# A gated attention/MLP decode step on one core: the first load of w1 split between two DMA queues

## The chip, the core and the metric

The kernel runs on one core of a Trainium2 chip. The core has TensorE (matmul), VectorE, ScalarE, GpSimd (POOL in the profile) and SyncE (SP), and 16 DMA engines that move data between HBM and SBUF. Two queues issue its loads: SyncE's (q1 in the profile) and ScalarE's (q10). The metric is the device time of one execution in microseconds (us), and of several executions the median.

## What is computed

One decode step for two sequences: attention over a cache of 4,096 keys for 32 heads of 128, a small ReLU MLP on the same input, and a sigmoid gate that mixes the two. All tensors are bf16. Cut to what matters:

```python
# A_x [2,1,512], k_cache and v_cache [2,32,4096,128], wq [512,4096], wo [4096,512]
# w1 [512,1376], w2 [1376,512], gate_w [512]
x = A_x
g = sigmoid((x * gate_w).sum(-1, keepdims=True))
q = (x @ wq) split into 32 heads
p = softmax(q . k_cache * 128**-0.5)
a = (p . v_cache) @ wo
b = relu(x @ w1) @ w2
return g * a + (1 - g) * b
```

The caches are 128 MiB of the 145 MB that are read; wq and wo are 4 MiB each, w1 and w2 some 1.4 MB each.

## The kernel before, in words

**SBUF.** The tensor `kv` has three regions of 64 KB in each of the 128 partitions (`NREG`, `REG`). Each of the two caches is cut into eight units of 8 MiB that fill one region; in a load of a unit each partition is one row of 65,536 B. The third region (`C`) holds, until the queries are made, the weights wq (32,768 B in each partition) and w1 (11,008 B in each partition: four of the 512 rows of w1, so that partition p has rows 4p to 4p+3), an identity matrix, and in its first three partitions x (two rows of 1,024 B) and gate_w (one).

**Order of the work.** `P` collects operations for each engine in lists; `emit` writes them out in order, each with its waits on semaphores ahead of it. A DMA adds 16 to its semaphore when all of it has landed. SyncE's list is: w1 (L235), wq (L236), the units k0 and k1 without waits, then k2 into region C (L250, after "pe_qh", "dve_setup" and "act_q", that is, once the weights there are used), and then one unit after the other, each waiting until the region that it goes into is free. The order of the units is k0 to k4, v0, k5, v1, k6, v2, k7, v3 to v7. v7 comes in two pieces (L246); w2's last 1,280 rows (L252) and wo in four pieces (L255) follow, and at the end the store of the output (L257). ScalarE's list begins with x (L233) and gate_w (L234); its only other load is w2's first 96 rows, of 1,024 B each (L663), during the v units.

**The start.** GpSimd makes the constants (L262 to L265). `gate` transposes x and gate_w on TensorE (L284, waits for both loads), ScalarE copies them to `xT32` (L287, the signal "act_xT"), four matmuls and a few small operations make the gate. `x_proj` (L340 to L378) waits for "act_xT", wq and w1 (L371) and multiplies x by wq and w1 in one loop on TensorE (L320 clears, L314 matmuls); its end is "pe_qh". VectorE and ScalarE put the queries into place ("act_q"), and GpSimd builds from them the weights for the key matmuls (`w_block`, L393). The key units wait for these: `k_turn` (L404) transposes a unit in place on VectorE once it has landed, and TensorE multiplies it (L314).

**The end.** `project` (L598) multiplies by wo piece by piece as it lands, VectorE and ScalarE cast the result (L623, L625), and SyncE stores it. `fill` puts operations without effect (increments of a semaphore that nobody waits for) into an engine's list ahead of `project`; they set how many instructions the engine has up to there.

**Blocks.** The program is emitted in two parts: a first few operations of SyncE, ScalarE and GpSimd (4, 2 and 4, the tuple `rest` at L700), then TensorE's whole list with its loops, then what is left of the others.

## Time and profile before

| | us |
|---|---|
| median of 3 runs (lowest to highest) | 342.52 (342.45 to 342.62) |
| the profiled execution, its own time | 342.64 |
| its span in the profile | 341.3 |
| busy: TensorE matmul / weight load | 209.9 / 33.9 |
| busy: VectorE / ScalarE / GpSimd | 155.4 / 13.9 / 41.8 |
| w1: from issue to landing | 5.8 |
| wq: from issue to landing | 15.0 |
| w2's first 96 rows: from issue to landing | 19.8 |

How to read the profile: times are microseconds from the span's start, L12 is line 12 of the kernel. A line of the timeline gives the start, the duration, the engine, the line, the operation and how many of it, and in brackets how long the engine was idle before it and what ended that. SPq and ACTq are the DMA queues of SyncE and ScalarE; their durations are those of the issue, not of the transfer. In the table by stretches, each engine's busy time and count is followed by the clock granted to TensorE, the share of the 16 DMA engines and GB/s. The trace also has a record of every DMA packet (queue, size, start, duration), without the number of the DMA engine that moved it.

### The profile page before, as it was taken

What the parts mean: (1) busy time and instruction counts of PE and PEld (TensorE: products, weight loads), DVE (VectorE), ACT (ScalarE), POOL (GpSimd) and SP (SyncE); (2) the same over time, 40 slices, a digit from 0 to 9 for tenths busy, and PEclk for the clock granted to TensorE, in tenths of its full rate; (3) what the DMA queues carried; (4) which work ended last, traced back from release to release, by engine and by line L of the source; (5) the groups of instructions that cost most, each with busy time, mean ns of one, the idle gap of its engine ahead of it and who ended that gap; (6) DMA issues with size and microseconds to landing.
All of it is one profiled execution on the core that took longest, in us unless ns stands there. A gap on an engine that the chain in (4) does not pass through costs nothing. (4 is left out here: it accounts for less than half of the span.)

```text
span 341.3 us, 3101 instructions
## 1 busy us (share of the span) xinstructions
PE 209.9 (61%) x1243; PEld 33.9 (10%) x843; DVE 155.4 (46%) x45; ACT 13.9 (4%) x37; POOL 41.8 (12%) x53
## 2 busy tenths in 40 slices
PE   0080079685968909972995059820993773718387
PEld 0040011000100101110111001100100100101024
DVE  1010897979799769229800693019805000000111
ACT  2001000000000020000000000000003000000000
POOL 1000000000000004005002300050000235050400
PEclk9999999999898965996799559965696659676789
DMA  8998989898999999998989898989999999999896
GB/s 346 434 492 369 492 369 492 369 492 369 492 392 468 399 461 445 415 484 376 492 369 492 369 492 369 492 369 492 392 468 392 468 438 424 398 441 461 374 440 264
DMA packets 3580, 145.46 MB, mean 426 GB/s; under 512 B 405, under 2 KB 634, under 8 KB 762
## 3 DMA queue, kind: packets, MB, share of 16 engines
q1 hardware_dynamic: 3460, 145.33, 98.7%
q10 hardware_dynamic: 118, 0.10, 0.1%
q8 instruction: 1, 0.02, 0.0%
q14 instruction: 1, 0.01, 0.0%
HBM read 145.43 MB, written 0.00 MB: 426 GB/s over the span
## 5 line engine op out<-in xcount | busy, mean ns | idle before, releaser
L404 DVE STREAM_TRANSPOSE kv<-kv 128x8192 uint32<-128x8192 uint32 (+1 forms) x17 | 138.6, 8186 | 74.4 <-DMA kv<-in_A_k_cache_dram 74.4
L314 PE MATMUL PS<-kv,zero 128*128 (+1 forms) x544 | 130.3, 421 | 40.4 <-PEq L481 40.4
L314 PE MATMUL PS<-kv,ptw 128*32 x512 | 48.1, 469 | 11.7 <-issue 11.5
L320 PE MATMUL PS<-zero 32*128 32x512 bf16 (+2 forms) x21 | 9.7, 537 | 57.6 <-ACT zero L410 20.3
L449 POOL TENSOR_TENSOR ptw<-E,mask 128x512 bf16<-128x512 bf16 x32 | 32.2, 1038 | 21.1 <-PE PS L314 10.9
L467 DVE TENSOR_TENSOR X<-PS,maskc 128x512 f32<-128x512 f32 x2 | 1.4, 692 | 64.1 <-PE PS L314 64.1
L314 PEld LDWEIGHTS PS<-kv,zero 128*128 (+1 forms) x144 | 13.6, 103 | 154.6 <-issue 154.6
L393 POOL TENSOR_TENSOR zero<-q_sb,mask 128x32 bf16<-128x32 bf16 x8 | 1.9, 251 | 147.0 <-PE PS L314 123.3
L471 POOL TENSOR_TENSOR X<-X,maskc 128x512 f32<-128x512 f32 x6 | 6.2, 1039 | 109.2 <-ACT X L470 109.2
L314 PE MATMUL PS<-X,zero 128*64 128x512 f32 x16 | 11.6, 819 | 12.3 <-PEq L481 12.3
L314 PEld LDWEIGHTS PS<-kv,ptw 128*32 x512 | 8.7, 99 | 50.4 <-issue 49.7
L320 PEld LDWEIGHTS PS<-zero 32*128 32x128 bf16 x21 | 2.1, 109 | 69.4 <-issue 43.7
L373 DVE STREAM_TRANSPOSE ptw<-PS 128x1024 f32<-128x1024 f32 x1 | 1.3, 1251 | 16.4 <-PE PS L320 16.4
L415 DVE TENSOR_REDUCE zero<-PS 128x2 f32<-128x2048 f32 x2 | 4.5, 2271 | 9.1 <-PE PS L314 9.1
L470 ACT ACTIVATE X<-PS 128x512 f32<-128x512 f32 x6 | 3.6, 597 | 71.4 <-PE PS L314 71.4
L422 ACT ACTIVATE nrow<-mmax 128x32 f32<-128x32 f32 x2 | 0.5, 228 | 132.8 <-DVE mmax L419 132.8
L440 DVE STREAM_TRANSPOSE E<-E 128x2048 bf16<-128x2048 bf16 x2 | 4.6, 2300 | 2.4 <-ACT E L430 2.4
L410 ACT ACTIVATE zero<-zero 1x1 f32<-1x1 f32 x9 | 1.8, 200 | 84.9 <-DMA kv<-in_A_v_cache_dram 67.9
L430 ACT ACTIVATE E<-PS,negm 128x1024 bf16<-128x1024 f32 x4 | 4.4, 1109 | 0.6 <-DVE negm L426 0.6
L284 PE MATMUL PS<-kv 3*128 3x3 bf16 x4 | 0.3, 165 | 6.5 <-DMA kv<-in_gate_w_dram 6.5
L598 PE MATMUL PS<-kv,oW 128*2 128x256 bf16 x64 | 4.0, 272 | 0.4 <-DMA kv<-in_A_wo_dram 0.4
L314 PEld LDWEIGHTS PS<-X,zero 128*64 (+1 forms) x16 | 1.8, 161 | 15.8 <-issue 15.6
(49 smaller groups left out, 27.6 us busy)
## 6 DMA issues: line engine op xcount, KB each, us to landing
kv<-in_A_v_cache_dram SPq DMA_DIRECT2D x1, 6144.0 KB, 36.7
kv<-in_A_wq_dram SPq DMA_DIRECT2D x1, 4096.0 KB, 15.0
kv<-in_A_wo_dram SPq DMA_DIRECT2D x1, 2560.0 KB, 35.9
kv<-in_A_v_cache_dram SPq DMA_DIRECT2D x1, 2048.0 KB, 41.3
kv<-in_B_w_dram SPq DMA_DIRECT2D x1, 1376.0 KB, 5.8
kv<-in_B_w_dram SPq DMA_DIRECT2D x1, 1280.0 KB, 30.1
kv<-in_A_wo_dram SPq DMA_DIRECT2D x1, 1024.0 KB, 37.9
kv<-in_A_wo_dram SPq DMA_DIRECT2D x1, 384.0 KB, 38.4
```

The costliest lines, as they stand in the source:

```text
L314: return e.add_instruction(mybir.InstMatmult(name=nc.get_next_instruction_name(), engine=mybir.EngineType.PE, ins=[rhs, lhsT], outs=[e.low ...
L320: return e.matmul(dst, lhsT=nil, rhs=nil.unsqueeze(1).to_broadcast([32, 4, 128]) if n == 512 else nil[:, 0:n], start=not stop, stop=stop, ...
L393: pool(lambda g: g.tensor_tensor(out=out, in0=q, in1=msk, op=ALU.mult), waits=([["act_q", "dve_mask8"], []] + [[f"pesc_{x}"] for x in rang ...
L404: ins = v.transpose(out=reg[:, 4096 * p0:4096 * p1], in_=reg[:, 4096 * p0:4096 * p1])
L410: return lambda a: a.activation(out=tick[:, 2 + i:3 + i], in_=tick[:, 0:1], func=ACT.Copy).then_inc(sem["go"], n)
L415: dve(lambda v: v.tensor_reduce(out=mpad[:, 0:2], in_=PSF[:, 0:2048].rearrange("p (x h q) -> p h x q", h=2, q=16), axis=AX.XY, op=ALU.max) ...
L430: act(lambda a, h=h: a.activation(out=E[:].rearrange("p (x h q) -> p h x q", h=2, q=16)[:, h], in_=PSF[:, 0:2048].rearrange("p (x h q) -> ...
L440: dve(lambda v: v.transpose(out=E[:], in_=E[:]), waits=[f"act_exp{b}"], signal=f"dve_et{b}")
L449: pool(lambda g, src=src, dst=dst: g.tensor_tensor(out=dst, in0=src, in1=msk, op=ALU.mult), waits=(([f"dve_et{b}"] if ub == 0 else []) + ( ...
L470: act(lambda e: e.activation(out=X2[:], in_=src, func=ACT.Copy), waits=[f"pe_v_{v}"], signal=f"act_x_{v}")
L471: pool(lambda e: e.tensor_tensor(out=X, in0=X, in1=msk, op=ALU.mult).then_inc(sem["xg"], 1), waits=[f"act_x_{v}"] + ([] if v else ["dve_se ...
L598: pe(lambda e, g=g: e.matmul(psf(64 * g, 64 * g + 2, FIN_C0, 256), lhsT=w, rhs=m[:, 256 * g:256 * g + 256], start=start, stop=stop, tile_p ...
```

## The change

w1 is loaded by two DMAs instead of one: ScalarE sends partitions 0 to 15, as the first thing in its list and so ahead of x and gate_w, and SyncE sends partitions 16 to 127 where it sent all 128. Both add 16 to w1's semaphore, so `x_proj` waits for 32. One `fill` operation of ScalarE goes, and ScalarE's first part has three operations instead of two.

```diff
+    for q, p0, p1 in ((act, 0, 16), (sp, 16, 128)):
+        q(lambda e, p0=p0, p1=p1: e.dma_start(w1_sb[p0:p1], B_w1.rearrange("(p t) f -> p (t f)", t=4)[p0:p1]).then_inc(sem["w1"], 16))
     act(lambda e: e.dma_start(x_sb[0:2], A_x.rearrange("b s d -> (b s) d")).then_inc(sem["x"], 16))
     act(lambda e: e.dma_start(x_sb[2:3], gate_w.rearrange("(o d) -> o d", o=1)).then_inc(sem["gw"], 16))
-    sp(lambda e: e.dma_start(w1_sb, B_w1.rearrange("(p t) f -> p (t f)", t=4)).then_inc(sem["w1"], 16))
     sp(lambda e: e.dma_start(wq_sb, A_wq.rearrange("(p t) n -> p (t n)", t=4)).then_inc(sem["wq"], 16))
...
-        pe(fn, dwaits=[(sem["wq"], 16), (sem["w1"], 16)], waits=["act_xT"], signal="pe_qh")
+        pe(fn, dwaits=[(sem["wq"], 16), (sem["w1"], 32)], waits=["act_xT"], signal="pe_qh")
...
-    fill("act", 5)
+    fill("act", 4)
...
-    rest = (("sp", nc.sync, 4), ("act", nc.scalar, 2), ("pool", nc.gpsimd, 4), ("dve", nc.vector, 0))
+    rest = (("sp", nc.sync, 4), ("act", nc.scalar, 3), ("pool", nc.gpsimd, 4), ("dve", nc.vector, 0))
```

## The prediction

> **What bounds the kernel now.** I read the page's slices first, then the DMA queues, the end of the chain, and last the first eight microseconds.

> ```profile
> DMA  8998989898999999998989898989999999999896
> GB/s 346 434 492 369 492 369 492 369 492 369 492 392 468 399 461 445 415 484 376 492 369 492 369 492 369 492 369 492 392 468 392 468 438 424 398 441 461 374 440 264
> ...
> q1 hardware_dynamic: 3460, 145.33, 98.7%
> q10 hardware_dynamic: 118, 0.10, 0.1%
> ```

> The 16 DMA engines are busy in every slice; only the first and the last move clearly less. SyncE's queue (q1) alone carries 145.33 MB. No compute engine comes near: TensorE is at 61%, VectorE at 46%. In the trace's packet records one row of 65,536 B takes 2,420 ns (27.08 GB/s per engine), one of 32,768 B 1,213 ns and one of w1's 11,008 B 413 ns. Adding up the records, no engine idles between 3.5 and 336 us. So the time is when the engines start, plus a fixed sum of rows, plus the tail. The tail, in the chain of work that ended last:

> ```profile
> 300.10 37.89 DMA kv<-in_A_wo_dram
> 337.99 0.04 issue
> 338.03 1.64 PE PS L598 x24
> 339.67 0.02 issue
> 339.69 0.41 DVE ptw L623
> ```

> wo's last pieces are waited for, then 24 matmuls, the cast and the store of the output follow. A DMA counts as landed only when all the engines that carry it are done, so the slowest of the 16 sets the end. Since every engine runs without a pause, a delay of the slowest engine at the start reaches the end whole. Hence only the start matters here, first by stretches (the last two columns are the share of the DMA engines and GB/s), then by its issues:

> ```profile
> 0.00:1.60 1.60, 0.00 (x0) 0.00 (x0) 0.00 (x0) 0.00 (x0) 0.84 (x7) 1.00 0.00 0
> 1.60:2.00 0.40, 0.00 (x0) 0.00 (x0) 0.00 (x0) 0.00 (x0) 0.40 (x1) 1.00 1.45 225
> 2.00:3.00 1.00, 0.00 (x0) 0.00 (x0) 0.58 (x4) 0.53 (x1) 0.39 (x1) 1.00 0.48 143
> 3.00:4.00 1.00, 0.00 (x0) 0.00 (x0) 0.70 (x4) 0.75 (x1) 0.00 (x0) 1.00 1.14 484
> ```

> ```profile
> 0.74 0.40 SPq L235 DMA_DIRECT2D kv<-in_B_w_dram  x1
> 0.74 0.54 ACTq L233 DMA_DIRECT2D kv<-in_A_x_dram  x1
> ...
> 1.19 0.42 SPq L236 DMA_DIRECT2D kv<-in_A_wq_dram  x1
> 1.31 0.23 ACTq L234 DMA_DIRECT2D kv<-in_gate_w_dram  x1
> ...
> 6.53 0.26 PE L284 MATMUL PS<-kv 3*128 3x3 bf16 x4 [6.53 <-DMA kv<-in_gate_w_dram]
> ...
> 16.28 1.03 PE L320 MATMUL PS<-zero 32*128 32x512 bf16 x3 [8.94 <-issue]
> ```

> Both queues issue at 0.74. Nothing moves before 1.6. A packet is counted where it starts, so the step from 143 to 484 GB/s means that most first rows are still running until 3 us. By the packet records x's two rows start at 1.67 and 1.68; w1's first rows start at 1.77 to 1.96 on eight engines and 2.2 to 2.73 on the others. Those first rows end between 2.60 and 3.27; from then on each engine puts 413 ns rows end to end. The slowest has w1's eight rows at 6.14. Had it begun with x (1.67) at full pace, its first row would have ended at 2.08: what there is to win is 3.27 - 2.08 = 1.19 us at most.

> **The change, part by part.**

> *Issues.* SyncE still issues one DMA for w1 (112 rows, not 128), so wq and the k units are issued where they were: 0.40 and 0.42 us, then L250. ScalarE issues one DMA more, by the nearest row 0.40 us; x moves to about 1.2 and gate_w to about 1.75, with no wait added. ScalarE's next work, the table load, starts at 2.47 anyway behind POOL's memset: nothing. One no-op fewer in ScalarE's last section keeps its count of instructions.

> *x and gate_w behind a row of w1.* ScalarE's only other load, w2's first 96 rows, shows how the queues mix: issued at 284.7, it appears as six rounds of one 1 KB row per engine, 2.49 us apart, so one row of each queue in turn. x and gate_w can thus lose some rows: 413 ns each beside w1, 1,213 ns beside wq. They have room. The gate runs from 6.53, its casted x is ready at 7.02, and x_proj waits for wq until 16.28: gate_w may come 16.28 - 7.02 = 9.3 us later, whereas the eight wq rows of one engine are 9.7 us. If it came behind all of them, x_proj would begin up to about 1 us later, and that is covered too: q is ready at 26, k0 lands at 35.5 (9 us of room), and the DMA that waits for q (k2, issued at 26.4) is not needed before k1 lands at 54.9. Zero; without this cover, 1 us. The doubled count on w1's semaphore adds nothing, since wq lands last.

> *The rows.* w1's 128 rows are eight per engine. w2's 96 rows came as six per engine. So 16 rows should be one per engine and 112 seven: still eight, 176,128 B from ScalarE plus the rest, no byte more. What changes is which engine writes which partitions. In a 128-row load each engine has eight partitions of its own; with six or seven rows per engine the shares can't coincide with these, so engines meet in one part of SBUF. No row shows two long rows meeting. The nearest is w2's load beside v7: each 1 KB row takes 46 to 52 ns and the 65,536 B row behind it is 20 to 33 ns longer in five of the six rounds, together some 75 ns, twice the 38 ns that 1,024 B take at 27.08 GB/s. [...] That reads as two writers sharing one way at half pace; that all engines show much the same stretch, in the first round only 9 to 16 ns, speaks for a cost of switching queues instead. I take the sharing, by that doubling.

> The bounds for ScalarE's 16 rows: 413 ns if nothing is shared; 8 x 413 = 3.3 us if partitions 0 to 15 have only two ways of eight. I take four writers to a way, between them: 4 x 413 = 1.65 us. SyncE's seven rows: 7 x 413 = 2.89 us with no meeting, 5.78 if each row meets one other; I take the middle, 4.34, for the slowest engine. Start at 1.70 (x's rows): 1.70 + 1.65 + 4.34 = 7.69 against 6.14, so **+1.55 us**. I let the slow first rows of today (0.52 us of stretch and 0.41 of idling, mean per engine) pass beneath the sharing; on top they give +2.5, and seven meetings give +3.0. With no meeting among the seven: 6.24, +0.1.

> [...]

> **Rivals.**

> *Nothing is shared, and ScalarE's short DMA fills the start (not slower).* For it: x's small DMA moved first, 0.10 us ahead of w1 and up to 1.06 ahead of the last engine. Each engine would do a row of 413 ns while SyncE's descriptors are still arriving, and its first SyncE row then ends no later than today's 2.60 to 3.27, with six left instead of seven: 0.41 us less, 342.1; at the very most 1.19 less, 341.3. It decides if a row of 11,008 B takes about 413 ns beside three others into partitions 0 to 15. Against it: first rows were slow on engines that had started early, too (up to 1,362 ns).

> *No net effect.* The engines' start is as slow with two queues, because the first rows wait for memory and not for the queue: 342.5. For it: the eight early and the eight late engines end their first rows in the same stretch. [...]

> **How the numbers follow.** The profiled execution took 342.64 us: span 341.3 and 1.3 around it. It lies 0.12 above the median of 342.52. 342.64 + 1.55 = 344.19 on its own time, 344.1 from the median. Chances: sharing that shows, 0.55 (own range 343.3 to 345.4, the top being 342.5 + 2.9); nothing shared, 0.30, of which 0.13 wins more than 0.2% (0.69 us, about what a measurement of this kernel can tell from no change) and 0.17 less; no net effect, 0.15. So faster 0.13, same 0.32, slower 0.55. The range must reach the rivals: 341.8 to 345.4.

> **What would show it.** In the profile after: w1's 11,008 B rows of ScalarE's queue at about 1,650 ns on all engines, SyncE's w1 rows at 413 or 826, the slowest engine through with w1 near 7.7 instead of 6.1, wq landing 1 to 2 us later than 15.0 after its issue, and the last wo matmuls about 1.5 us later with the tail unchanged. Rows of 413 ns throughout, and GB/s in 2 to 3 us far above 143, would make me wrong; so would a gate that starts after 26 us, or an engine idle after 3.5.

## The result and the profile after

The changed kernel takes 345.37 us (median of 6 runs, 345.06 to 345.82) against 342.57 us (342.45 to 342.74): 2.80 us more, a ratio of 1.0081 with a 95% interval of 1.0070 to 1.0091. Slower was forecast, with 344.1 us.

The profiled execution took 345.54 us, its span is 344.2, so the 1.3 us around it have stayed and the loss lies within. The stretches of the start, from the profile after (last two columns: share of the DMA engines, GB/s):

```profile
1.60:2.00 0.40, 0.00 (x0) 0.00 (x0) 0.00 (x0) 0.00 (x0) 0.40 (x1) 1.00 2.27 330
2.00:3.00 1.00, 0.00 (x0) 0.00 (x0) 0.58 (x4) 0.53 (x1) 0.38 (x1) 1.00 0.33 110
3.00:4.00 1.00, 0.00 (x0) 0.00 (x0) 0.70 (x4) 0.75 (x1) 0.00 (x0) 1.00 1.44 231
```

From 3 us on, where 484 GB/s were counted before, it is 231. The same table for 1.6 to 9 us as a whole, first of the kernel before:

```profile
1.60:9.00 7.40, 0.53 (x8) 0.39 (x8) 1.45 (x8) 2.05 (x5) 0.79 (x1) 1.00 1.01 403
```

and after:

```profile
1.60:9.00 7.40, 0.00 (x0) 0.00 (x0) 1.28 (x7) 1.28 (x1) 0.78 (x1) 1.00 1.07 262
```

The engines' share is as high as before (1.07 and 1.01), so they are not waiting for work: each has a row in hand, and the rows move at two thirds of the rate. The busy share alone does not show the loss here; the GB/s beside it (262 and 403) do. In the timeline after, the consequences downstream:

```profile
0.74 0.39 SPq L235 DMA_DIRECT2D kv<-in_B_w_dram  x1
0.74 0.42 ACTq L235 DMA_DIRECT2D kv<-in_B_w_dram  x1
...
1.19 0.53 ACTq L236 DMA_DIRECT2D kv<-in_A_x_dram  x1
...
10.32 0.26 PE L286 MATMUL PS<-kv 3*128 3x3 bf16 x4 [10.32 <-DMA kv<-in_gate_w_dram]
...
19.23 1.03 PE L322 MATMUL PS<-zero 32*128 32x512 bf16 x3 [8.10 <-issue]
```

The gate starts 3.8 us later than before (10.32 against 6.53) and still has its room. x_proj, which waits for wq, starts at 19.23 instead of 16.28. The DMA issues show the same (KB, us from issue to landing), after:

```profile
kv<-in_A_wq_dram SPq DMA_DIRECT2D x1, 4096.0 KB, 18.0
```

By the packet records the slowest engine is through with w1 at 8.79 us instead of 6.14, so **2.65 us** later; the first wq row of each engine is stretched, too (1,413 to 1,731 ns, not 1,213), and wq ends at 18.69 instead of 15.82 (+2.87). From there the distance stays: k0 ends 2.9 us later, the last of wo 3.0. The end of the chain, after:

```profile
338.58 2.35 PE PS L600 x40
340.93 0.04 issue
340.98 1.62 PE PS L600 x24
342.59 0.03 issue
342.62 0.41 DVE ptw L625
```

The last 24 matmuls begin at 340.98 instead of 338.03 and take as long as before.

### The profile page after: what moved, and what is told of

Read it like the earlier page. It is cut to its first block, busy times and chain, and to the rows that moved or that the text cites. A ratio compares the mean times of both kernels' runs of the same rounds, so it can differ in the third digit from the quotient of the medians.

```text
span 344.2 us, 3101 instructions
## 1 busy us (share of the span) xinstructions
PE 208.8 (61%) x1243; PEld 33.8 (10%) x843; DVE 155.4 (45%) x45; ACT 13.9 (4%) x37; POOL 41.8 (12%) x53
## 5 line engine op out<-in xcount | busy, mean ns | idle before, releaser
L316 PE MATMUL PS<-kv,ptw 128*32 x512 | 47.0, 458 | 12.9 <-issue 12.8
```

The costliest lines, as they stand in the source:

```text
L316: return e.add_instruction(mybir.InstMatmult(name=nc.get_next_instruction_name(), engine=mybir.EngineType.PE, ins=[rhs, lhsT], outs=[e.low ...
```

## The experiments

Theory A: an engine that writes into partitions which another engine is filling shares one way into SBUF with it, and both go slower ("way" stands for whatever it is that they share). Rival B: two queues that feed the same engines disturb each other at the start. Rival C: the cost comes from the memory side, the extra DMA or the narrow shape. All kernels below start from the kernel before; `w1_in` is w1 as `(p t) f -> p (t f)`, and w1's semaphore is awaited to 32 where two DMAs add to it. Differences are between medians, against the runs of the kernel before on the same chip (342.56 to 342.65).

### The queue or the partitions: sp_both and columns

```diff
 # sp_both
+    for p0, p1 in ((0, 16), (16, 128)):
+        sp(lambda e, p0=p0, p1=p1: e.dma_start(w1_sb[p0:p1], w1_in[p0:p1]).then_inc(sem["w1"], 16))
 # columns
+    act(lambda e: e.dma_start(w1_sb[:, 0:688], w1_in[:, 0:688]).then_inc(sem["w1"], 16))
     act(lambda e: e.dma_start(x_sb[0:2], ...
+    sp(lambda e: e.dma_start(w1_sb[:, 688:], w1_in[:, 688:]).then_inc(sem["w1"], 16))
```

> w1 still in 16 and 112 rows, but both from SyncE's queue, ScalarE as before the change. Theory A (rows of several engines meet on one way into SBUF): the queue doesn't matter, w1's rows are stretched to 500 to 1,500 ns again and the time is 2.3 to 3.1 us above before (344.9 to 345.7). Theory B (two queues that feed the same engines disturb each other at the start): the time goes back to before, 342.4 to 342.8.

> ScalarE sends an eighth of w1 ahead of x again, but as the first 1,376 B of all 128 rows; SyncE sends the other 9,632 B of all 128. Bytes, queues and order as in the changed kernel, each engine stays with its own eight partitions. Theory A: no stretch beyond the first rows, 342.0 to 342.9 (eight more packets of some 8 ns per engine; perhaps a fuller start). Theory B: 344.5 to 345.5, as in the changed kernel.

sp_both: 344.82 us, +2.21 (ratio 1.0063, 1.0050 to 1.0077). columns: 342.72 us, +0.11 (1.0003, 0.9994 to 1.0012). The stretch from 1.6 to 9 us, first of sp_both:

```profile
1.60:9.00 7.40, 0.53 (x8) 0.39 (x8) 1.45 (x8) 2.05 (x5) 0.79 (x1) 1.00 1.08 328
```

and of columns:

```profile
1.60:9.00 7.40, 0.00 (x0) 0.00 (x0) 1.28 (x7) 1.28 (x1) 0.79 (x1) 1.00 1.02 403
```

One queue with the split by partitions loses; two queues with a split by columns, the same bytes and the same order, move 403 GB/s as before. B falls as the cause of this loss. sp_both came out 0.1 below its expected range and 0.6 below the changed kernel, so where the 16 rows stand in the order has some weight. columns also answers the hope behind the other rival: ScalarE's first row starts at 2.76 us, a microsecond behind SyncE's (1.75), and there is no gain.

### The 16 rows alone: copies into spare space

Here w1 is loaded whole as before, and its first 16 rows (176 KB) once more, into space that nothing reads. This leaves the 112 rows out of the question and costs one row of bytes per engine, 0.41 us.

```diff
+    spare = kv[:, C, 22528:28032]
+    act(lambda e: e.dma_start(spare[0:16], w1_in[0:16]).then_inc(sem["w1"], 16))       # copy_16
+    act(lambda e: e.dma_start(spare[0:128:8], w1_in[0:16]).then_inc(sem["w1"], 16))    # copy_16_apart
+    act(lambda e: e.dma_start(spare[0:32:2], w1_in[0:16]).then_inc(sem["w1"], 16))     # copy_16_pairs
+    act(lambda e: e.dma_start(spare[:, 0:688], w1_in[0:16].rearrange("p (c f) -> (p c) f", c=8)).then_inc(sem["w1"], 16))  # copy_128
```

> The kernel before, and ScalarE loads the first 16 rows of w1 a second time, ahead of x, into spare space of partitions 0 to 15. These are 176 KB more, one row of 413 ns per engine, so at least +0.41 us. Theory A with four engines to a way: 4 x 413 = 1.65 us, so 344.0 to 344.6. Theory B: +0.41 and whatever two queues cost, which is the same for this kernel and the next one.

> As copy_16, but the 16 rows go to every eighth partition (0, 8, ... 120) instead of 0 to 15; HBM addresses, queue, row length and number of rows are the same. [...] Theory B, and any cause on the side of HBM or of the descriptors: the same time as copy_16.

> Control for the copies: the same 176 KB of w1 a second time from ScalarE ahead of x, but laid out as 1,376 B in each of all 128 partitions. Theory A: bytes alone, 0.41 to 0.6 us above before (343.0 to 343.3). If the extra bytes themselves, or an extra DMA ahead of x, made copy_16's 2.83 us: 345.

> copy_16 with the 16 rows in every second partition (0, 2, ... 30). How large is a way? [...] If a way is eight partitions in a row, four meet: 344.2 to 344.6, and copy_16 had eight (3.3 us), copy_16_apart none.

| kernel | partitions | us | difference | ratio, 95% |
|---|---|---|---|---|
| copy_128 | all, 1,376 B each | 343.12 | +0.56 | 1.0017, 1.0008 to 1.0027 |
| copy_16_apart | every 8th | 343.56 | +0.95 | 1.0026, 1.0017 to 1.0036 |
| copy_16_pairs | every 2nd of 0 to 30 | 343.72 | +1.16 | 1.0037, 1.0023 to 1.0050 |
| copy_16 | 0 to 15 | 345.44 | +2.83 | 1.0080, 1.0067 to 1.0094 |

Queue, HBM addresses and bytes are the same in all four. The moment is not: by the packet records the copied rows start at 2.73 us in copy_16 and at 2.82 in copy_128, but only at 5.16 in copy_16_apart and 5.33 in copy_16_pairs, where ScalarE's issue took 0.58 and 0.59 us instead of 0.41. So copy_128 and copy_16, which move at nearly the same moment, are the pair to compare: the extra DMA and its bytes cost 0.56 us over all partitions (rows of 1,376 B) and 2.83 in 16 neighbouring ones (rows of 11,008 B). How much of the distance from copy_16 to copy_16_apart is owed to the partitions and how much to the moment, these two don't tell; no run has separated rows that move at 2.7 us. And copy_16 costs well over 1.65 us, the author's estimate for four engines to a way.

### Away from the start: copy_16_late and copy_16_apart_late

The same two copies, issued by ScalarE behind the copy that gives "act_xT", into the stream of wq.

```diff
     act(lambda a: a.activation(out=xT32[:, :, 0:3], ... signal="act_xT")
+        act(lambda e: e.dma_start(spare[0:16], w1_in[0:16]).then_inc(sem["w1"], 16))       # or spare[0:128:8]
```

> copy_16 with its DMA issued by ScalarE only after x is transposed (at about 7 us), into the running stream of wq. Theory A with four to a way and no help from the slow start: 1.65 us (344.3), and up to copy_16's 2.8 if the owners of the ways are held up as well. If copy_16's cost belongs to the start (first rows, filling of the queues): 0.41 to 0.6 above before (343.0 to 343.2).

> copy_16_late with the 16 rows in every eighth partition, the cleanest pair without the start. [...] No meeting: 343.0.

copy_16_late: 344.27 us, +1.71 (1.0052, 1.0038 to 1.0065). copy_16_apart_late: 343.68 us, +1.03 (1.0031, 1.0019 to 1.0043). The first is near the author's estimate of four engines to a way, 4 x 413 ns = 1.65; the second is 0.62 above the 0.41 us of its bytes. Here the moment is the same, too (the first copied row starts at 10.59 us in both), so the 0.68 us between them belong to the partitions; the row length and the narrow shape are the same in both, and with that C falls. The two intervals overlap a little; the single runs lie at 344.23 to 344.46 and 343.52 to 344.24 (the trace of the second is of its slowest, 344.24). The view by stretches, where the copies pass, first of the kernel before:

```profile
10.00:11.00 1.00, 0.00 (x0) 0.00 (x0) 0.00 (x0) 0.00 (x0) 0.00 (x0) 1.00 1.21 524
11.00:13.00 2.00, 0.00 (x0) 0.00 (x0) 0.00 (x0) 0.00 (x0) 0.00 (x0) 1.00 0.72 311
13.00:14.20 1.20, 0.00 (x0) 0.00 (x0) 0.00 (x0) 0.00 (x0) 0.00 (x0) 1.00 1.01 437
```

and of copy_16_late:

```profile
10.00:11.00 1.00, 0.00 (x0) 0.00 (x0) 0.00 (x0) 0.00 (x0) 0.00 (x0) 1.00 0.68 209
11.00:13.00 2.00, 0.00 (x0) 0.00 (x0) 0.00 (x0) 0.00 (x0) 0.00 (x0) 1.00 1.01 246
13.00:14.20 1.20, 0.00 (x0) 0.00 (x0) 0.00 (x0) 0.00 (x0) 0.00 (x0) 1.00 1.02 437
```

Less from 10 to 13 us, then 437 GB/s as before: the loss is local, and no later row repairs it. In the packet records the 16 rows themselves take only 413 to 819 ns. The wq row of 32,768 B **behind** each takes 1,918 to 2,324 ns instead of 1,213; the two together are 2.67 to 2.74 us on every engine, 1.1 more than 413 + 1,213. So most of the added time is not written at the 16 rows but at the rows next behind them. In copy_16 it is written at the rows of w1 behind: the 16 that start between 4.0 and 5.2 us take 1,340 to 1,628 ns each instead of 413.

### The 112 rows: copy_112 and late_16

```diff
 # copy_112: rows 16 to 127 once more, into spare space, ahead of x
+    act(lambda e: e.dma_start(spare[16:128], w1_in[16:128]).then_inc(sem["w1"], 16))
 # late_16: the change's two parts, but ScalarE's DMA stands behind "act_xT"
+    sp(lambda e: e.dma_start(w1_sb[16:128], w1_in[16:128]).then_inc(sem["w1"], 16))
+        act(lambda e: e.dma_start(w1_sb[0:16], w1_in[0:16]).then_inc(sem["w1"], 16))
```

> The other part of the change by itself: the kernel before, and ScalarE loads the rows 16 to 127 of w1 a second time, ahead of x, into spare space of partitions 16 to 127. Seven rows per engine are 2.89 us of bytes. Theory A: the seven meet too; the model with two writers at half pace gives 4.5 to 6.9 above before (347.1 to 349.5). If only the 16 rows in 16 partitions do harm: 2.9 to 3.1 above before (345.5 to 345.7).

> SyncE's 112 rows of w1 start alone, as in the changed kernel; ScalarE sends the 16 rows only after x is transposed, into the stream of wq. No byte is loaded twice. If both parts of the change do harm: copy_16_late showed 1.71 - 0.41 = 1.30 us for 16 rows in the stream, and the seven rows per engine add 1.0 to 1.7, so 344.8 to 345.7. If the 112 rows are harmless by themselves: 343.8 to 344.0.

copy_112: 348.49 us, +5.93 (1.0172, 1.0159 to 1.0186). The bytes are 2.89 of it, 3.0 us are left: the seven rows per engine do harm, too. late_16: 346.45 us, +3.80 (1.0111, 1.0096 to 1.0126), more than expected and more than the changed kernel. Its packet records separate the parts: with the 112 rows alone at the start the slowest engine ends at 7.30 us. At full pace seven rows would have ended one row before the 6.14 of the kernel before, at 5.72; so the 112 rows cost 1.58 us more than at full pace. With the 16 rows behind them wq ends 3.34 later than before. Why these cost so much more there than in copy_16_late I did not separate.

### Another cut, and two full queues: halves and act_w1

```diff
 # halves
+    act(lambda e: e.dma_start(w1_sb[0:64], w1_in[0:64]).then_inc(sem["w1"], 16))      # ahead of x
+    sp(lambda e: e.dma_start(w1_sb[64:128], w1_in[64:128]).then_inc(sem["w1"], 16))
 # act_w1: w1 whole, from ScalarE ahead of x; SyncE begins with wq
+    act(lambda e: e.dma_start(w1_sb, w1_in).then_inc(sem["w1"], 16))
```

> The split put elsewhere: ScalarE sends partitions 0 to 63 ahead of x, SyncE 64 to 127. [...] If only narrow transfers (16 rows) do harm: 342.4 to 342.9.

> w1 whole, but from ScalarE ahead of x, while SyncE begins with wq: two queues feed all engines from the start, each with all 128 partitions. Theory A: no loss, 342.2 to 342.9, and a gain of up to 0.4 if two queues fill the start better. Theory B: above 343.5.

halves: 346.55 us, +3.90 (1.0111, 1.0096 to 1.0127), far above the 342.4 to 342.9 expected if only narrow transfers did harm: 64 partitions do, too. From 1.6 to 9 us it has (the trace is of its slowest execution, 347.72 us):

```profile
1.60:9.00 7.40, 0.00 (x0) 0.00 (x0) 1.28 (x7) 1.28 (x1) 0.79 (x1) 1.00 1.09 237
```

act_w1: 343.05 us, +0.40 (1.0015, 1.0005 to 1.0024). Two full queues from the start do not hurt nearly as a split by partitions does, and do not help: 0.15 above the time expected at most, 0.45 below B's. In its packet records the rows of both queues mix from 4.3 us to the end of w1, and all w1 rows there take 413 ns, all wq rows 1,213: two queues at once cost no row anything there, with both loads on all 128 partitions. None of the twelve kernels is faster than the kernel before; columns, the nearest, can't be told from it.

## Why the prediction was right, and where it was not

- **What bounds the kernel.** Right. The slowest engine's 2.65 us in w1 and 0.2 in wq came out at the end as 2.9 us of span, and no engine idled between 3.5 and 336 us in either trace.
- **Issues, x and gate_w.** Right. ScalarE's issue took 0.42 us, x and gate_w went out at 1.19 and 1.75, and the gate ran at 10.32, with 8.9 us to go before x_proj.
- **ScalarE's rows start with x's, at 1.70.** Wrong. The DMA was issued at 0.74 like x before, yet its first row starts at 2.73, behind one SyncE row on each engine; in columns it is 2.76, in copy_16 2.73.
- **Today's slow first rows pass beneath the sharing.** Wrong, and this is the mis-sized term. SyncE's rows still come first, and the first on each engine take 413 to 1,724 ns (before 411 to 1,362). In the kernel before, the slowest engine needs 6.14 - 1.77 - 8 x 0.413 = 1.06 us more than its rows. Put on top: 1.77 + 1.06 + 1.65 + 4.34 = 8.82, and 8.79 was measured; against 6.14 that is +2.68, with 0.2 of stretched wq rows +2.9. The text had this as its variant "on top" (+2.5).
- **The size and the range.** 1.55 us were forecast and 2.80 came. The range held by 0.03 us (345.37 under 345.4), and three of the six runs lie above its top; that it held is owed to the variants beside the sum, "on top" and "seven meetings", and is luck in part.
- **Sharing by half, for two writers.** Right in direction: the same rows at the same moment in neighbouring or separated partitions differ by 0.68 us in the stream (1.71 and 1.03). That two writers go at half pace each was the author's estimate from w2's stretched rows; no run shows how many engines write to one way at a time. The 1.88 us between copy_16 and copy_16_apart don't show it, since their rows move 2.4 us apart. The text took w2's stretched rows for sharing and named a cost of switching queues as the other reading; act_w1, where the rows of two queues mix and keep their 413 and 1,213 ns, speaks for its choice. (The 65,536 B rows beside w2's are v6's, not v7's; v7's rows have 49,152 and 16,384 B and begin at 305.87.)
- **Four to a way for the 16 rows, 1.65 us.** Near in the stream (copy_16_late, 1.71). At the start the copy cost 2.83; the 1.1 us between the two were not explained. The four is an estimate between one and eight that no run shows: the runs showed these two costs in its place, and no count of engines. That the rows share one way into SBUF is itself inferred from such sizes; what the runs show is that the partitions decide. The sum above closes with 1.65 nonetheless, but it has only one total to fit, so it does not prove that the terms fall out like this.
- **Seven rows, 4.34 us.** Near: late_16 gives 7.30 - 1.77 - 1.06 = 4.47.
- **What would show it.** The slowest engine was through later than the 7.7 named, wq landed 3.0 later and not 1 to 2. ScalarE's rows were to take 1,650 ns each; they take 413 to 1,325, and the SyncE rows right behind them up to 1,484. Whoever had looked only at the rows named would have called the theory wrong.
- **How large a way is.** Not shown. copy_16_pairs and copy_16_apart, which move their rows at nearly the same moment (5.33 and 5.16 us), came out close to each other (+1.16 and +0.95), and copy_16_pairs (343.72) below the 344.2 to 344.6 expected for ways of eight partitions in a row.

That each engine has the same eight partitions in every load of 128 rows, and takes neighbouring rows of the 112, remains an inference from the counts and the times: the records have no engine numbers. What makes the first rows of each engine slow (411 to 1,362 ns in the kernel before), the memory or descriptors still on their way, was not shown. What the start adds to copy_16 stays open as well, and so does why some copies start to move only at 5.2 us.

## What to carry to other kernels

## What the runs showed beyond that

- In the kernel before, late in the stream, the rows of the two queues take turns: w2's 96 rows of 1,024 B took six rounds of 16, 2.49 us apart, with one 65,536 B row of SyncE's on each engine between each two. At the start that isn't so: gate_w's row, issued at 1.31, moved only at 5.60, when w1 was nearly through.
- A DMA of ScalarE's, issued at 0.74 us like SyncE's, has its first packet at 2.73 to 2.82 us with 16 neighbouring, 112 or (as parts of rows) 128 partitions, and at 5.16 and 5.33 with 16 separated ones; SyncE's first is at 1.75 to 1.77 in these kernels. x's two rows alone had theirs at 1.67.
- Splitting w1 into halves (+3.90 us) cost more than 16 and 112 rows (+2.80).
